# Loading v through GpSimd's casting queue into two padded operands, and one more half batch in seven products

## The chip, the cores and the metric

The kernel runs on one core of one Trainium2 chip. The metric is the device time of one execution in microseconds (us); smaller is better. The kernel before was timed three times: 272.16, 272.57 and 272.89 us, median 272.57 us. One further execution was recorded by the hardware profiler, and all profile lines in this document come from such recordings.

## The reference

Two layers follow each other. The first is a linear attention with cosine and sine weights over 8 batches, 8 heads, 576 positions and 64 values for each head. The second is a two-matrix network with a squared ReLU.

```python
q_p, k_p = phi(q), phi(k)                  # relu(x)*cos(pos) beside relu(x)*sin(pos): 64 -> 128 values
kv  = einsum('bhsf,bhsd->bhfd', k_p, v)    # sums over the 576 positions
z   = sum(k_p, axis=2)
num = einsum('bhsf,bhfd->bhsd', q_p, kv)
den = einsum('bhsf,bhf->bhs', q_p, z) + 1e-06
x   = (num / den) as [4608 tokens, 512]
out = (relu(x @ w_in) ** 2) @ w_out        # 512 -> 2048 -> 512
```

Inputs and output are float32. On the chip the matrix products take bfloat16 and sum in float32.

## The kernel before, in words

**Staging.** A batch has 512 main positions (four blocks j of 128) and a tail of 64. For each batch, q and k are loaded as float32 into one buffer `kq`. VectorE (DVE) or ScalarE (ACT) makes the features, eight instructions for each batch (cos and sin for four blocks j, q and k at once); `fe` holds them in bfloat16. TensorE sums the products of the key features with v in `mm_kv`; its second operand is v with a column of ones beside each head's 64 values (so z comes out with kv), padded to 66 columns: `vext` for the main positions, `vextt` for the tails. The sums are copied to `kvz`. The query features are turned by DMA transposes (`qT_dma`), `mm_num` multiplies them with `kvz`, `div` divides, and DMA transposes (`x_dma`) turn the result into `xT`, the network's input. Batches 0 and 1 are turned by TensorE instead.

**The network.** A batch's 512 main tokens are taken in two halves of the 2048 hidden columns, `gg` 0 and 1, each of two groups `s` of 256. Each can be done plainly (`plan_plain1`: four products `H<batch>.<group>.<token half><hidden half>` of eight matmuls for each group, in which a product needs one token half of `xT` only) or in seven products (`plan_gemm1`: `G<batch>.<group>.P1` to `P7` of four matmuls each). The seven products work on sums of input blocks (`xs`, DVE) and of weight blocks (`w1s`), and each group has seven evictions from PSUM (`seed`, `u2`, `s5`, `c11`, `c12`, `c22`, `c21`) where the plain form has four. P1 needs both token halves. A pair of output blocks is made in seven products as well (`Y<batch>.P1` to `P7`). Before, `PLAIN` names three halves for the plain form: both of batch 1, and the first of batch 2. The tails of all batches are the ninth block, `G8` and `Y8`.

**v before.** For batches 3 to 7, SyncE's queue (SP) loads v as float32 into a staging buffer (`vs`, one slot, in two halves of four heads, in rows of 1 KB; `vst` for the tail). Then ACT or DVE casts each half into the single `vext` (`spread_v`, operations `vs<batch>.0` to `.2`). Batch 2 is loaded by GpSimd's queue (POOL), which can cast, into a bfloat16 staging buffer, and copied to `vext`. As there is one `vext`, the spread of a batch waits until the sums of the batch before have read it.

**Order.** A long table (`ORDER`) gives one order of all operations; each engine and each queue runs its own operations in that order and waits where it must. A star puts an operation on ACT. A planner in the kernel (`Plan.run`) goes through the table with a cost for each operation and picks buffers; the table itself was made outside. Operations of the table that matter here: `ldk`, `ldq`, `ldv` (loads), `kv<b>` (the sums of batch b), `qTd<b>.<i>` and `xTd<b>.<i>` (DMA transposes on SP), `sin<b>.<j>` and `cos<b>.<j>` (features).

The end of the kernel is `Y8`: the last product `P21`, one copy `c111` of 128x256 from PSUM by DVE, and two small stores, one by SP and one by ACT's queue.

Of the kernel before, what the change touches and what calls it, by code (L numbers as in the profile page):

```python
# [35 lines left out]
xT1.2 xTc1.2 Y0.a12 ldk2 Y0.a13 Y0.a14 Y0.b12 Y0.b13 w2t3 xT1.0 xTc1.0 Y0.a15 xTc1.1* vs2.0*
num1.3 Y0.b14 div1.3 Y0.c01* Y0.b15 Y0.c10* Y0.c11 Y0.c00* cos2.1 ldqt3 sin2.0 H1.3.00.0 sin2.1
cos2.3 xT1.3 xTc1.3* sin2.3 ldqt2 H1.3.00r* H1.2.00.0 H1.2.00r* ldkt2 H1.2.10.0 ldv2.1 vs2.1
H1.1.10.0 H1.1.11.0 H1.1.00.0 cos2.0* sin2.2* H1.0.11.0 H1.1.11r* H1.0.01.0 cos2.2* H1.1.00r*
ldkt3 sin2.tk* H1.2.10r* H1.3.10.0 H1.0.11r H1.3.10r* H1.2.01.0 Y0.st1 H1.1.10r* H1.0.01r  # L40
cos2.tk kv2 w2t2 w2t4 H1.1.11q H1.3.10q* kvz2* H1.2.01r* H1.0.10.0 H1.0.10r Y0.st0 qTd2.0
H1.1.01.0 H1.1.01r H1.1.10q H1.3.00q* H1.0.00.0 H1.0.00r* qTd2.1 num2.1 div2.1 H1.2.11.0
H1.3.11.0 ldv3.0 num2.2 H1.2.11r* ldv3.2 H1.1.00q* H1.3.01.0 H1.3.11r* H1.1.01q H1.3.01r* Y1.P10
ldk3 vs3.2* div2.2 H1.3.11q H1.3.01q ldq3 num2.3 div2.3 Y1.seed Y1.P11 Y1.S1 Y1.seed1 Y1.P20
num2.0 div2.0 vs3.0* Y1.P21 Y1.c111* Y1.S2 Y1.S3 cos3.1* ldv4.2 Y1.P5 cos3.0 sin3.0* sin3.1
sin3.2 xTd2.1 num1.4 cos3.3* Y1.P6 H2.1.10.0 Y1.u2 H2.0.11.0 sin3.3* cos3.2 H2.1.10r* Y1.P7
div1.4 ldv3.1 H2.0.11r* Y1.S4 vs4.2* vs3.1* xT1.4 xTd2.0 xs2.1 H2.0.00.0 xs2.3 H2.1.00.0 xs2.2
kv3 xTc1.4* H2.0.01.0 H2.1.00r xs2.4 Y1.c110* H2.0.00r* H2.1.00q* Y1.s5* G2.2.P1 H2.0.01r* kvz3
Y1.c22 G2.2.seed qTd3.0 num3.0 div3.0 cos3.tq* sin3.tq H2.1.11.0 H2.1.11r* H2.1.11q H2.0.10.0
H2.0.10r* num3.1 qTd3.1 H2.1.01.0 div3.1 Y1.P3 num3.2 H2.1.10q* ldq4 w1s3 G2.2.P2 Y1.c12  # L50
H2.1.01r* H2.1.01q* G2.2.P6 G2.2.c11r* div3.2 ldv4.0 G2.2.u2 G2.2.P5 G2.3.P1 ldk4 num3.3 div3.3
vs4.0* qTd3.2 ldkt4 G2.3.P5 G2.2.P7 G2.3.seed G2.2.s5* G2.2.c22r xTd3.0 G2.3.P2 G2.3.P6 G2.3.s5*
G2.3.P3 ldv4.1 G2.2.P4 G2.2.P3 G2.3.u2 G2.3.c11r* G2.3.P7 cos4.3 num3.4 G2.3.c11q Y2.P1 cos4.0
sin4.1* G2.2.c21r* G2.3.c22r G2.2.c12r sin4.0 cos4.1* cos4.2* G2.3.P4 G2.3.c21r xTd3.1 ldv5.2
G2.3.c12r sin4.2 xs3.1 sin4.3* ldkt5 Y1.st0 Y1.P4 Y2.seed G2.3.c21q* G2.3.c22q* G2.3.c12q Y2.S1
G3.0.P1 G3.0.seed qTd4.0 Y1.c21* qTd4.1 Y2.P2 G3.0.P2 xs3.2 G3.0.c11r* G3.0.P5 xs3.3 G3.1.P1
G3.0.P6 G3.0.s5* cos4.tk* G3.1.P5 Y2.S2 G3.0.u2* div3.4 G3.0.P3 Y2.P6 sin4.tk* vs4.1 kv4
G3.0.c12r Y2.u2 G3.1.seed G3.1.P2 Y2.S3 ldk5 G3.1.P6 vs5.2* kvz4* Y2.c11* Y2.S4 G3.0.P7 num4.0
G3.0.c22r ldv5.0 G3.1.c11r* G3.1.c11q* Y2.P5 xs3.4 G3.0.P4 G3.2.P1 div4.0 ldq5 G3.1.u2* G3.1.s5*
ldqt5 vs5.0* Y1.st1 G3.0.c21r num4.2 div4.2 G3.1.P3 Y2.s5 G3.1.P7 G3.1.c22r G3.1.c12r Y2.P7  # L60
num4.1 div4.1 ldqt6 G3.2.seed ldv5.1 G3.1.P4 G3.1.c21r* G3.2.P6 G3.2.u2* ldqt4 G3.2.P2 G3.2.c11r
sin5.0 Y2.c22 Y2.P3 Y2.c12 cos5.3* num4.3 G3.2.P5 G3.3.P1 G3.3.P5 cos5.1* xTd4.0 div4.3 xTd4.1
G3.2.s5* G3.3.seed G3.2.P7 G3.2.c22r G3.2.P3 G3.2.c12r sin5.1 G3.3.s5* G3.3.P6 Y2.st0 G3.3.u2*
cos5.0 qTd5.0 G3.3.P2 G3.3.c11r* G3.3.c11q G3.2.P4 G3.3.P3 G3.3.P7 Y2.P4 G3.3.c22r vs5.1* sin5.3
cos5.2 G3.1.c12q* G3.3.P4 Y3.P1 G3.1.c21q* G3.3.c21r G3.3.c12r G3.3.c12q sin5.2* kv5 xs4.1
G3.2.c21r* G3.3.c21q xs4.2 G4.0.P1 G4.0.P5 qTd5.1 ldv6.0 G3.3.c22q* Y3.seed Y3.P2 cos5.tq*
sin5.tq* kvz5* G3.1.c22q Y3.S1 Y3.S2 xs4.3 num5.0 div5.0 xs4.4 G4.0.seed G4.0.P2 G4.0.s5* ldv6.2
G4.0.P3 Y2.c21* G4.1.P1 G4.0.c11r* G4.0.P6 G4.0.u2* G4.0.c12r ldk6 Y3.S4 Y3.P6 ldq6 G4.1.seed
G4.1.P2 G4.1.c11r* G4.0.P7 G4.1.P6 G4.1.u2* G4.0.c22r vs6.2* num5.2 Y3.S3 G4.1.P5 G4.2.P1
Y3.c11* G4.0.P4 G4.1.P7 G4.1.s5* div5.2 Y3.P5 G4.1.c22r G4.1.c22q num5.3 div5.3 G4.1.P4 G4.1.P3  # L70
G4.0.c21r* G4.1.c12r Y3.u2* G4.2.seed G4.2.P6 G4.2.P2 vs6.0* G4.1.c21r* num5.1 G4.2.u2*
# [12 lines left out]
Y4.c22 G5.3.P1 G5.3.seed num5.4 cos7.0 G5.2.P7 Y4.P3 sin7.1 G5.2.c22r Y4.c12 G5.3.P2 G5.3.c11r*
G5.3.P6 G5.3.u2 div5.4 vs7.1 G5.3.P5 G5.2.P4 xTd6.0 xTd6.1 G6.0.P1 ldv7.2 G5.3.s5* G5.3.P7
G5.3.c22r G5.3.P3 G5.1.c21q* G5.3.c12r Y4.P4 G5.2.c21r* G5.3.P4 G5.1.c12q sin7.3* vs7.2*
G6.0.seed Y4.c21 xs6.1 xs6.2 kv7 G6.0.P2 G6.0.P5 G6.1.P1 kvz7 qTd7.0 num7.0 xs6.3 xs6.4 G6.0.P6
G5.3.c11q* G6.0.s5* G6.0.P3 G6.1.seed G6.1.P2 G6.1.P6 G5.3.c21r* G6.0.c11r* div7.0 G6.1.c11r
G6.0.u2* G6.0.c12r G5.3.c12q* num7.1 Y5.P1 sin7.tq qTd7.1 G6.1.P5 div7.1 G6.1.u2 G6.0.P7
G6.0.c22r xTd5.2 num7.2 div7.2 G6.2.P1 G5.3.c21q* Y5.seed G6.1.s5* G5.3.c22q* Y5.P2 Y5.S1 Y5.S2  # L90
Y4.st0 G6.0.P4 G6.1.P7 G6.0.c21r Y4.st1 Y5.c11* G6.1.c22r cos7.tq qTd7.2 num7.3 G6.1.P3 div7.3
Y5.P5 G6.1.c12r G6.2.seed G6.2.P2 G6.2.c11r* G6.2.P6 xTd7.1 Y5.S4 xTd7.0 Y5.S3 G6.1.P4 G6.2.u2*
Y5.s5* G6.2.P5 G6.1.c21r* G6.2.s5* Y5.P6 G6.3.P1 G6.2.P7 Y5.u2* Y5.P3 G6.2.P3 G6.1.c22q*
G6.3.seed G6.3.P6 G6.3.P2 G6.3.c11r* G6.2.c22r G6.1.c21q Y5.P7 G6.3.u2* G6.3.P5 G6.2.c12r
G6.3.P7 G6.3.c11q Y5.c12 G6.2.P4 G7.0.P1 G6.1.c11q G6.3.s5* G6.3.P3 Y5.c22 Y5.P4 G6.3.c22r
G6.3.c22q G6.3.c12r G6.3.P4 xs7.1 G6.2.c21r* xs7.2 G7.0.seed G7.0.P2 G7.0.c11r xs7.3 Y6.P1
Y5.st0 Y5.c21 xs7.4 G7.0.P5 G7.1.P1 G7.0.s5 G6.1.c12q* G6.3.c12q* Y6.S1 G6.3.c21r* G6.3.c21q*
# [185 lines left out]
def kernel(  # L283
# [189 lines left out]
    def att_bufs(b):  # L473
        kq[b] = buf("kq", [P, 2, H, J, D], F32, "kq")
        vtype = BF16 if b < 3 else F32
        for i in range(2):
            vs[b, i] = buf("y" if b == 1 else "vs", [P, HH, J, D], vtype, "vs")
# [1144 lines left out]
```

## Time and profile before

| | |
|---|---|
| median of three runs | 272.57 us |
| profiled execution, its own time | 271.95 us |
| span of the profiled execution | 269.9 us |
| TensorE busy in the span | 263.1 us, 97% |
| VectorE, ScalarE, GpSimd busy | 228.1, 186.7, 26.9 us |
| granted TensorE clock | 1.0 |

The span is the time between the first and the last instruction; the profiled execution's own time is 2.05 us longer. Queues are written as engine names with a q: SPq is the queue that SyncE issues into. In the page's strips the span is cut into 40 slices of 6.75 us, and a digit is the busy share in tenths. A group's row gives the instruction, what it writes and reads, how often it runs, its busy time with the mean of one in ns, and the idle time just before it. A DMA row gives the time from issue to landing. The matmul of 256 columns has a duration of 273 ns, but matmuls overlap: sixteen that follow each other take 1.75 us in the chain of work, 0.109 us each.

### The profile page before, as it was taken

Reading aid. Unit: us, or ns where it says so; the run is one execution under the profiler, and the core shown is the slowest. Engines: PE = TensorE matmul, PEld = TensorE weight load, DVE = VectorE, ACT = ScalarE, POOL = GpSimd, SP = SyncE. Lnnn points to the kernel's source line nnn. Section 1 sums busy time; section 2 is a strip of 40 time slices with the busy share of each in tenths; the row PEclk is TensorE's granted clock in tenths of the full one; section 3 lists DMA queues with packets and bytes.
Section 4 is the critical chain, followed back from the end, with each engine's and each line's share of the span. In section 5 each row is a group of like instructions: output and inputs, shape, how many; then the busy total and the mean of one; then the engine's idle time right before and its main releaser. Section 6 shows DMA issues by size and latency. Waiting matters only on the chain.

```text
span 269.9 us, 6751 instructions
## 1 busy us (share of the span) xinstructions
PE 263.1 (97%) x2787; PEld 225.0 (83%) x2792; DVE 228.1 (85%) x412; ACT 186.7 (69%) x289; POOL 26.9 (10%) x44
## 2 busy tenths in 40 slices
PE   8899999999999999999999999999999999999994
PEld 3568856699899889989998998899888888888883
DVE  3877987889998999999999999899978858797941
ACT  4762695698888997689699868587658636755510
POOL 8934443200000000000000000000000000000000
PEclk9999999999999999999999999999999999999999
DMA  6999999999899999999899998652540111010115
GB/s 221 220 206 253 328 198 250 298 295 298 221 247 314 221 261 298 300 183 231 284 275 209 232 359 208 152 155 100 61 125 15 38 63 78 8 72 2 78 50 186
DMA packets 82367, 51.23 MB, mean 190 GB/s; under 512 B 53217, under 2 KB 78817, under 8 KB 82337
## 3 DMA queue, kind: packets, MB, share of 16 engines
q1 hardware_dynamic: 71008, 38.28, 55.5%
q0 software_dynamic: 10736, 12.00, 21.2%
q10 hardware_dynamic: 592, 0.52, 0.6%
q8 instruction: 22, 0.36, 0.6%
q14 instruction: 9, 0.07, 0.1%
HBM read 36.70 MB, written 9.44 MB: 171 GB/s over the span
## 4 chain that ended last, share of the span: by engine, by line
PE 83%; DMA 12%; POOL 3%; issue 0%; DVE 0%; POOLq 0%
PE ya L461 18%; PE yb L461 16%; PE hb L461 13%; PE ha L461 8%; PE hc L461 8%; PE hps L461 8%; DMA w1sb<-in_moe_w_in_dram 5%; DMA kq<-in_k_dram 4%; PE num L461 3%; DMA w2sb<-in_moe_w_out_dram 3%; PE kz L461 3%; PE yc L461 3%; PE yh L461 3%; POOL kq L509 1%; POOL w1sb L411 1%; POOL v L1378 1%
## 5 line engine op out<-in xcount | busy, mean ns | idle before, releaser
L461 PEld LDWEIGHTS <-w1sb 128*128 128x128 bf16 x736 | 70.4, 98 | 8.6
L461 PEld LDWEIGHTS <-gs 128*128 128x128 bf16 x512 | 49.9, 98 | 5.8
L461 PEld LDWEIGHTS <-gT 128*128 128x128 bf16 x448 | 43.1, 98 | 9.8 <-issue 0.2
L442 ACT ACTIVATE gT<-gT 128x1024 bf16<-128x1024 bf16 x38 | 39.5, 1059 | 3.4 <-DVE gT L455 1.8
L461 PE MATMUL hps<-xT,w1sb 128*128 128x256 bf16 x320 | 37.4, 273 | 0.0
L448 ACT ACTIVATE fe<-kq,cols 128x1024 bf16<-128x1024 f32 (+1 forms) x39 | 35.1, 950 | 2.8 <-DMA kq<-in_k_dram 1.7
L461 PEld LDWEIGHTS <-w1s 128*128 128x128 bf16 x312 | 29.7, 98 | 3.3
L461 PE MATMUL ya<-w2sb,gT 128*128 128x256 bf16 x256 | 30.7, 273 | 0.0
L461 PE MATMUL hb<-xs,w1sb 128*128 128x256 bf16 x208 | 30.6, 273 | 0.0
L450 DVE TENSOR_SCALAR fe<-kq,cols 128x1024 bf16<-128x1024 f32 (+1 forms) x41 | 26.9, 690 | 4.0 <-DMA kq<-in_k_dram 4.0
L461 PE MATMUL ha<-xT,w1sb 128*128 128x256 bf16 x176 | 26.2, 273 | 0.0
L444 DVE TENSOR_TENSOR gT<-gT 128x1024 bf16<-128x1024 bf16 x34 | 23.2, 686 | 1.2 <-ACT gT L436 0.8
L436 ACT ACTIVATE gT<-ha 128x512 bf16<-128x512 f32 x21 | 12.6, 601 | 15.9 <-PE ha L461 15.9
L633 DVE TENSOR_TENSOR xp<-num,den 128x512 bf16<-128x512 f32 (+1 forms) x33 | 22.2, 675 | 1.1
L436 ACT ACTIVATE gT<-hps 128x512 bf16<-128x512 f32 x26 | 15.4, 602 | 8.1 <-PE hps L461 8.0
L455 DVE CUSTOM_DVE_ANT_0 gT<-hb,s 128x512 bf16<-128x512 f32 x26 | 17.8, 686 | 3.7 <-PE hb L461 3.3
L458 DVE TENSOR_TENSOR gs<-gT 128x2048 bf16<-128x2048 bf16 x16 | 19.4, 1219 | 0.4
L455 DVE CUSTOM_DVE_ANT_0 gT<-hc,u 128x512 bf16<-128x512 f32 x26 | 17.7, 683 | 0.8 <-PE hc L461 0.8
L432 ACT COPY hb<-ha 128x512 f32<-128x512 f32 x26 | 15.2, 585 | 4.3 <-DVE gT L438 1.8
L461 PE MATMUL hb<-xs,w1s 128*128 128x256 bf16 x104 | 15.6, 273 | 0.0
L436 ACT ACTIVATE gT<-hb 128x512 bf16<-128x512 f32 x18 | 10.8, 599 | 7.0 <-PE hb L461 4.5
L461 PE MATMUL hc<-xs,w1s 128*128 128x256 bf16 x104 | 15.6, 273 | 0.0
(120 smaller groups left out, 415.7 us busy)
## 6 DMA issues: line engine op xcount, KB each, us to landing
out_dram<-y SPq DMA_DIRECT2D x16, 512.0 KB, 3.7
vs<-in_v_dram SPq DMA_DIRECT2D x10, 512.0 KB, 4.8
kq<-in_k_dram SPq DMA_DIRECT2D x5, 1024.0 KB, 7.1
kq<-in_q_dram SPq DMA_DIRECT2D x5, 1024.0 KB, 9.2
w1sb<-in_moe_w_in_dram POOLq DMA_DIRECT2D x4, 512.0 KB, 11.6
w2sb<-in_moe_w_out_dram POOLq DMA_DIRECT2D x4, 512.0 KB, 10.3
kq<-in_q_dram POOLq DMA_DIRECT2D x2, 1024.0 KB, 11.2
kq<-in_k_dram POOLq DMA_DIRECT2D x2, 1024.0 KB, 11.1
```

The source lines that it names most:

```text
L411: nc.gpsimd.dma_start(out=w1sb[:, :, f0:f1], in_=moe_w_in[:, f0:f1].rearrange("(kb p) f -> p kb f", p=P),)
L432: (nc.scalar.copy if e == "ACT" else nc.vector.tensor_copy)(out=out, in_=in_)
L436: nc.scalar.activation(out=out, in_=in_, func=ACTF.Relu)
L442: nc.scalar.activation(out=out, in_=in_, func=ACTF.Square)
L444: nc.vector.tensor_tensor(out=out, in0=in_, in1=in_, op=ALU.mult)
L448: nc.scalar.activation(out=out, in_=in_, func=ACTF.Relu, scale=col)
L450: nc.vector.tensor_scalar(out=out, in0=in_, scalar1=0.0, scalar2=col, op0=ALU.max, op1=ALU.mult)
L455: nc.vector._custom_dve(dve_ops.TENSOR_ADD_SAT, out=out, in0=in0, in1=in1, s0=BIG, s1=0.0)
L458: nc.vector.tensor_tensor(out=out, in0=in0, in1=in1, op=op)
L461: nc.tensor.matmul(out=out, lhsT=lhsT, rhs=rhs, start=start, stop=stop, skip_group_check=True)
L509: eng.dma_start(out=kq[b][:, "kq".index(nm)][:, hs, js], in_=main_of(nm, b)[:, hs, js])
L633: nc.vector.tensor_tensor(out=x, in0=n4[:, :, :, 0:D].rearrange("p b (k l) d -> p b k l d", l=2), in1=r.rearrange("p b (k l) -> p b k l", l=2)
```

## The change

- v of batches 2 to 7 is no longer staged. GpSimd's queue reads float32 from HBM and writes bfloat16 straight into the padded operand. A half is now two blocks j with all heads, one DMA for each block (128 partitions, 8 heads, 64 values), so a half is two DMAs. The tail goes into `vextt` in the same way.
- There are two main operands, `vext0` and `vext1`, used in turn as the planner gives them. The staging pool is gone, and with it the 18 spreads `vs2.0` to `vs7.2`.
- `PLAIN` loses (2, 0): the first hidden half of batch 2 runs as `G2.0` and `G2.1`, in seven products.
- The last copy `c111` is cut in two: columns 0 to 127 on DVE (`c111l`), 128 to 255 on ACT (`c111r`); both stores wait for both.
- The second-matrix sum `w2t1` waits for two of the four weight loads instead of four.
- The table is new throughout. SP's queue has 43 plain DMAs instead of 58 (its 30 transposes stay), GpSimd's 62 instead of 35. The tail loads of q and k of batches 2 and 3 change places too.

```diff
-PLAIN = ((1, 0), (1, 1), (2, 0))
+PLAIN = ((1, 0), (1, 1))
...
-    pool("vs", 1, 4096)
...
-    plan.pool("ve", 1)
+    plan.pool("ve", 2)
...
+    vxs = [
+        sb.tile([P, J, H, E1 + 1], BF16, name=f"vext{i}", tag=f"vx{i}", bufs=1) for i in range(2)
+    ]
+    vx = vxs[0]
...
     def load_v(b, i, eng):
-        if i < 2:
+        if b > 1:
+            if i < 2:
+                for j in (2 * i, 2 * i + 1):
+                    src = main_of("v", b)[:, :, j]
+                    eng.dma_start(out=vxs[ve[b].slot][:, j, :, 0:D], in_=src)
+            else:
+                src = v[b, :, MAIN:S, :].rearrange("h p d -> p h d")
+                eng.dma_start(out=vxt[sides[b % 2], b % 2, :, 0:D], in_=src)
+        elif i < 2:
             src = main_of("v", b)[:, i * HH : (i + 1) * HH]
...
-                f"ldv{b}.{i}",
-                {eng: 0.6 if eng == "SP" else 0.95},
+                f"ldv{b}.{i}",
+                {"POOL": 2.0 if i < 2 else 0.95},
...
+            if last and t:
+                h = n // 2
+                parts = [
+                    ("l", {"DVE": dve(h)}, slice(0, h)),
+                    ("r", {"ACT": act(h)}, slice(h, n)),
+                ]
```

The two tables around the point where batch 2 enters the network (before, then after):

```
... num2.0 div2.0 vs3.0* Y1.P21 Y1.c111* Y1.S2 Y1.S3 cos3.1* ldv4.2 Y1.P5 cos3.0 sin3.0* sin3.1
sin3.2 xTd2.1 num1.4 cos3.3* Y1.P6 H2.1.10.0 Y1.u2 H2.0.11.0 sin3.3* cos3.2 H2.1.10r* Y1.P7
div1.4 ldv3.1 H2.0.11r* Y1.S4 vs4.2* vs3.1* xT1.4 xTd2.0 xs2.1 H2.0.00.0 xs2.3 H2.1.00.0 ...

... num2.0 div2.0 sin3.3* Y1.P21 Y1.c111* Y1.S2 Y1.P5 sin3.0* ldv3.0 w1s3 Y1.c110* cos3.1* num1.4
div1.4 Y1.P6 xT1.4 Y1.u2* xTd2.1 cos3.0* xTd2.0 sin3.1 G2.0.P1 G2.0.seed xTc1.4 xs2.1 xs2.2 xs2.4
sin3.2 cos3.3* Y1.P7 ldv4.0 ldqt3 cos3.2 G2.0.P6 G2.0.u2* G2.0.P5 G2.0.P2 xs2.3 G2.0.P7 ...
```

More of the change, by code (lines that the diff above doesn't have):

```diff
@@ L42 @@
[L42 to L59, printed above, removed]
@@ new lines @@
+w2t3 H1.2.00r* H1.1.11q* H1.0.01.0 H1.0.01r* Y0.st0 H1.3.10.0 H1.1.01r* H1.3.10r* w2t2 H1.3.00r*
+H1.0.00.0 kv2 H1.1.10r* H1.1.00.0 H1.1.01q w2t4 kvz2* H1.3.10q H1.0.00r H1.3.00q* qTd2.0 num2.1
+div2.1 qTd2.1 H1.1.10q H1.1.00r* H1.1.00q* Y1.S3 H1.2.01.0 H1.2.01r* H1.3.11.0 H1.3.11r*
+H1.2.11.0 H1.2.11r* num2.2 div2.2 H1.3.01.0 H1.3.01r* H1.3.01q* Y1.P10 Y1.seed H1.3.11q num2.3
+div2.3 ldq3 ldk3 Y1.P11 ldv4.2 Y1.P20 ldqt2 Y1.S1 Y1.seed1 num2.0 div2.0 sin3.3* Y1.P21 Y1.c111*
+Y1.S2 Y1.P5 sin3.0* ldv3.0 w1s3 Y1.c110* cos3.1* num1.4 div1.4 Y1.P6 xT1.4 Y1.u2* xTd2.1 cos3.0*
@@ new lines @@
+xTd2.0 sin3.1 G2.0.P1 G2.0.seed xTc1.4 xs2.1 xs2.2 xs2.4 sin3.2 cos3.3* Y1.P7 ldv4.0 ldqt3
+cos3.2 G2.0.P6 G2.0.u2* G2.0.P5 G2.0.P2 xs2.3 G2.0.P7 G2.0.s5 G2.0.P3 G2.0.c22r G2.0.c12r
+G2.0.c11r* G2.1.P1 G2.1.seed Y1.S4 G2.0.P4 Y1.s5 G2.1.P5 G2.1.s5* G2.1.P2 G2.1.c11r* G2.1.c11q
+G2.1.P6 G2.1.u2* ldv3.1 G2.0.c21r* kv3 kvz3* qTd3.0 G2.1.P7 G2.1.c22r G2.1.P3 cos3.tq* num3.0
+div3.0 qTd3.1 ldk4 sin3.tq* G2.2.P1 G2.1.c12r G2.2.P5 G2.1.c22q* G2.1.P4 ldq4 G2.1.c21r* num3.1
+div3.1 G2.2.seed qTd3.2 Y1.c22 Y1.P3 Y1.c12 G2.2.P2 num3.2 div3.2 G2.1.c12q* G2.1.c21q ldv5.2
@@ L474, in att_bufs @@
         kq[b] = buf("kq", [P, 2, H, J, D], F32, "kq")
-        vtype = BF16 if b < 3 else F32
-        for i in range(2):
-            vs[b, i] = buf("y" if b == 1 else "vs", [P, HH, J, D], vtype, "vs")
-        vs[b, 2] = buf("xpt" if b < 2 else "kqt", [P, HH if b < 2 else H, D], vtype, "vst")
+        ve[b] = buf("ve", None, None, "ve")
+        if b < 2:
+            for i in range(2):
+                vs[b, i] = buf("y", [P, HH, J, D], BF16, "vs")
+            vs[b, 2] = buf("xpt", [P, HH, D], BF16, "vst")
         if b < 2:
@@ L729, in spread @@
                     f"vs{b}.{i}",
-                    both(act(n), d) if i < 2 or b > 1 else both(0.6, 0.3),
+                    both(act(n), 0.06 + 0.0003 * n) if i < 2 else both(0.6, 0.3),
                     lambda e, i=i: spread_v(e, b, i),
-                    [landed[i]] + ([sums_of[max(1, b - 2)]] if i == 2 and b > 1 else []),
-                    [vs[b, i]] + ([] if i == 2 and b > 1 else [ve]),
+                    [landed[i]],
+                    [vs[b, i], ve[b]],
                 )
@@ L1344, in plan_w2_sums @@
                 lambda e, n=n, in0=in0, in1=in1: tt(w2t[n][:, :, :], in0(), in1(), ALU.subtract),
-                w2_in + [made[a] for a in after] + (plain if n == 3 else []),
+                w2_in[: 2 if n == 1 else 4]
+                + [made[a] for a in after]
+                + (plain if n == 3 else []),
             )
@@ L1557 @@
             if b + 1 < B:
-                got, ve = ahead.pop() if ahead else plan_loads(b + 1, "POOL" if b == 1 else "SP")
+                got = ahead.pop() if ahead else plan_loads(b + 1, "POOL" if b == 1 else "SP")
                 if b % 2:
```

226 lines of the change are left out of this document (114 added, 112 removed).

## The prediction

> **What bounds the kernel now.** I read the page's busy times first, then the chain of work, then the sixteen-matmul rows of the chain, to see how full the bounding engine is.
>
> ```profile
> span 269.9 us, 6751 instructions
> PE 263.1 (97%) x2787; PEld 225.0 (83%) x2792; DVE 228.1 (85%) x412; ACT 186.7 (69%) x289; POOL 26.9 (10%) x44
> DMA  6999999999899999999899998652540111010115
> PE 83%; DMA 12%; POOL 3%; issue 0%; DVE 0%; POOLq 0%
> ```
>
> TensorE ends the chain, and VectorE and ScalarE put nothing into it. The DMA share of the chain lies in the first 43 us (weights and the first batches). The DMA strip is full to slice 23, about 158 us. The stage from 60 to 80 us, where the plain half of batch 2 stands, looks so (busy by engine; chain; SyncE's queue; ScalarE):
>
> ```profile
> 60.00:80.00 20.00, 20.00 (x250) 17.99 (x249) 19.44 (x34) 17.01 (x26) 0.00 (x0) 1.00 0.96 255
> ...
> 74.92 0.66 PE yb L461 x6
> 75.57 1.75 PE hps L461 x16
> 77.32 1.75 PE yb L461 x16
> 79.06 0.22 PE tx L656 x4
> ...
> 70.06 1.26 SPq L678 DMA_TRANSPOSE xT<-xp  x1
> 71.43 0.53 SPq L526 DMA_DIRECT2D vs<-in_v_dram  x1
> 72.20 2.20 SPq L678 DMA_TRANSPOSE xT<-xp  x1
> ...
> 71.75 4.27 ACT L448 ACTIVATE fe<-kq,cols 128x1024 bf16<-128x1024 f32 x4
> ```
>
> TensorE has no gap there; VectorE is at 19.44 of 20. Sixteen matmuls take 1.75 us, 0.109 each. So work taken from VectorE and ScalarE buys nothing by itself: only fewer matmuls do, or a shorter end. New waits cost at once, because nothing covers TensorE.
>
> **The change part by part.** *The seven products.* The plain half has 2 groups x 4 products x 8 = 64 matmuls; in seven products it is 2 x 7 x 4 = 56. Eight fewer at 0.109 us: -0.87 us, all on the path. This is the only large saving.
>
> *The spreads.* These rows and the two bfloat16 copies of batch 2 go:
>
> ```profile
> L432 ACT CAST vext<-vs 128x1024 bf16<-128x1024 f32 x6 | 6.3, 1049 | 0.0
> L432 DVE CAST vext<-vs 128x1024 bf16<-128x1024 f32 x4 | 2.7, 685 | 0.0
> L432 ACT CAST vextt<-vst 64x512 bf16<-64x512 f32 x5 | 3.1, 614 | 0.1
> ```
>
> About 14 us of two engines that are not on the chain: 0. It pays for the seven products' evictions: 14 instead of 8 in the half, six more at 0.59 (ACT) to 0.69 us (DVE), 3.5 to 4.1 us, of which the ones that TensorE waits for count. In G2.0 the new order puts P5, P2, P7, P3 in a row, and P3 needs P5's bank copied out: cover 2 x 0.44 = 0.87 us, copy 0.69 plus two handoffs. Bounds: 0 (the rows of the seven-product groups show no idle TensorE) to one uncovered copy in each of two groups, 1.4 us. I take 0.3, nearer the rows.
>
> *The loads of v.* Before, a half is 512 rows of 1 KB on SP's queue; after, it is 2 x 128 x 8 = 2048 pieces of 256 B read and 128 B written, on GpSimd's queue. No row shows this transfer (none writes rows 132 B apart), but the tail loads of v at the start write 128 B pieces with a cast. The DMA view of 7.2 to 7.8 us:
>
> ```profile
> DMA packets 487, 0.11 MB, mean 178 GB/s; under 512 B 461, under 2 KB 476, under 8 KB 487
> q0 software_dynamic: 487, 0.11, 177.3%
> ```
>
> 0.6 us x 16 engines / 487 = 20 ns a packet by rate; 1.77 of them overlap, so 35 ns each if they did not. A half costs 2048/16 x 20 = 2.5 us by rate, at most 4.5. A half before is 512 KB; hardware packets average 0.555 x 269.9 x 16 / 71008 = 34 ns for all sizes, so 512/16 x 34 = 1.1 us or somewhat more. For a batch: about 5.0 instead of 2.2 to 3, some 2 to 3 us more on DMA engines that are full until 158 us. GpSimd's issue is free (its `kq` loads of as many pieces take 0.92 us each, and it has nothing else to do). Two operands let v come a batch earlier, so kv itself should not wait for v: batch 2's last half is issued near 48 us, behind k and q (k landed at 53.4), and 2.5 + 0.6 + 2.5 us later is 59, before kv2 (60.3, and 0.87 later in the new order). What matters is what these packets push back. After kv2 GpSimd is free to issue three halves (v3 twice, v4), 7.5 us, together with k3 and q3 on SP and just before xTd2.
>
> *Where batch 2 enters.* Before, the first product needs one token half (xTd2.1) and the other is first read at 79.29. After, G2.0.P1 follows Y1.P6 and the four tail transposes, and needs both. Arrival: 74.92 + 0.66 + 0.22 = 75.8 us. The two landings before:
>
> ```profile
> xT<-xp SPq DMA_TRANSPOSE x1, 2.8
> ...
> xT<-xp SPq DMA_TRANSPOSE x1, 4.9
> ...
> kq<-in_q_dram SPq DMA_DIRECT2D x1, 1024.0 KB, 9.2
> ```
>
> The later one was issued at 72.20 and landed at 77.1, behind the load of v that stood between them and now doesn't. If it lands as the first, 75.0: no wait. If as before, 1.3 us. Ahead of it in time are k3 and q3 (2 x 2.2, at 34 ns for each KB) and 7.5 us of v, all from about 61 us: until 73 or 74 at full use, so it competes with the last of them. I take 0.8 (bounds 0 and 1.3, more if v costs 4.5 a half, see below). There is a rule on this: the Trainium skill, "DMA: Bandwidth & Descriptors", section "Issuing engines are not separate DMA queues", says that the DMAs of all issuing engines run on the same 16 DMA engines and interleave. By that rule the 0.8 stands; were the queues separate paths, it would be 0 and the sum -0.3. The strip of before cannot tell the two apart.
>
> *The features of batch 3* move ahead of Y1's evictions on ScalarE: sin3.3, c111, sin3.0, c110, cos3.1, u2. Y1.P7, now right after G2.0.P1 (76.2), needs u2. q3 landed at 61.93 + 9.2 = 71.1; three features at 1.07, two copies at 0.37, u2 at 0.59 give 75.7. Covered by 0.5 us, so 0; each us that q3 lands later than 71.6 is a us of TensorE. Two loads of v less stand ahead of it on SP, three halves more on the other queue.
>
> *The end.* c111 on DVE was 0.42 us:
>
> ```profile
> 264.95 2.19 ACTq L1106 DMA_DIRECT2D out_dram<-y  x3
> 266.09 0.42 DVE L432 COPY y<-ya 128x256 f32<-128x256 f32 x1 [0.45 <-PE ya L461]
> ```
>
> ScalarE's part must stand behind that queue's second store, which was being issued until about 266.5, as DVE's copy ended. ACT copies 256 columns in 0.375 and 512 in 0.587 us, so 128 in about 0.27. The last stores go 0.26 later instead of 0.13 earlier (DVE's half alone). I take +0.26.
>
> *SP's queue* loses 15 issues of about 0.5 us in front of transposes, and the moved tail loads are 0.6 each: 0, no row has TensorE waiting for an issue there. Later batches: G3.0.P1 stands behind xTd3.1, which followed a v load that is gone from its queue, with 5 more us of v on the other: 0, bounds 0 and 2. w2t1, second memset: 0, the weights land as before.
>
> Sum: -0.87 + 0.3 + 0.8 + 0.26 = +0.5 us. On the profiled execution's own 271.95 that is 272.4; it lies 0.6 below the median of 272.57, on which I put it: 273.1 us.
>
> **The rivals.** *The packets are the bound (slower).* If 128 B pieces at 132 B steps cost 35 ns, three halves take 13.4 us; with 4.4 of k3 and q3 from 61 us they end near 79, and xTd2.0 with them: TensorE waits about 3 us instead of 0.8, and perhaps again after kv3, where four more such loads are issued beside k4 and q4. For it: the full strip to 158 us. Against: overlap of 1.77 in the row. 275 us, up to 277. It decides from about 27 ns a packet.
>
> *ScalarE's head of line, or the lock between VectorE and GpSimd (slower).* q3 at 73 instead of 71.1 costs 1.4 us through u2. And this row says that GpSimd's issue can hold VectorE:
>
> ```profile
> L450 DVE TENSOR_SCALAR fe<-kq,cols x14: 467/484/977, 5.0 to 40.4; 128x512 bf16<-128x512 f32 x14
> ```
>
> One feature took 977 instead of 484 ns, at the start, where GpSimd issues without pause. Two or three such in the 60 to 80 us stage, where VectorE has 0.56 us to spare, give 1 to 1.5 us. Either: 273.9 to 274.5. The Trainium skill, "SBUF — State Buffer", section "Who interferes with whom", makes it a rule: a VectorE operation in a two-port mode and a GpSimd operation block each other for a whole instruction. Against it stands where the issues fall: mostly after kv2, kv3, kv4, while the features follow later.
>
> *Faster.* The load of v that stood before xTd2.0 is gone, the transpose lands by 75.0, no group waits: -0.87, and with the end at +0.26 or -0.13 it is 271.6 to 272.0. It decides from xTd2.0 landing before 75.8. Against: three halves of v in flight just then.
>
> **How the numbers follow.** A difference of about 0.3% (0.82 us) is what a measurement of this kernel can tell from no change. Forecast, the saving eaten by small waits: 0.43, 272.0 to 273.4. Packets: 0.22, 274 to 277. ScalarE's line 0.12 and the lock 0.10, 273.4 to 274.5. Faster by over 0.3%: 0.13, as all waits must vanish and the end too must not grow. So slower 0.44, same 0.43, faster 0.13. The range 271.9 to 275.3 leaves out the best of the faster case and the worst of the packets.
>
> **What would show it.** TensorE's matmuls 8 fewer; `hps` 256, `ha`, `hb`, `hc` more. An idle TensorE ended by the transpose before the first `ha` of batch 2, near 76 us: 0.8. No idle at kv2 to kv7. v's landings 5 to 6 us after issue, 128 B packets near 20 ns by rate. The last DVE and ACT copies 0.4 us apart. The forecast is wrong if TensorE waits for `kq` features or kv, if DVE features above 750 ns are many, or if packets overlap less than in the row above.

## The result and the profile after

The changed kernel takes 281.24 us (median of four; 280.67 to 281.91) against 272.37 us (four runs of the kernel before beside it, 272.02 to 272.89): 1.033 times the time, interval 1.031 to 1.036. That is 8.9 us more than before; 273.1 had been forecast, with 275.3 as the upper end of the range. In the runs further down the median counts every execution, and the ratio leaves out those that lie more than 1.5% above the fastest of their kernel.

The page of the changed kernel, the lines that answer to those of before (span, busy time, the DMA strip, the chain of work, and one group of part 5):

```profile
span 278.8 us, 6744 instructions
PE 265.9 (95%) x2784; PEld 225.0 (81%) x2784; DVE 228.2 (82%) x409; ACT 179.5 (64%) x282; POOL 49.8 (18%) x71
DMA  7999999999996999999999999358114211200106
PE 90%; DMA 4%; DVE 4%; ACT 1%; issue 0%
L464 PE MATMUL ha<-xT,w1sb 128*128 128x256 bf16 x192 | 29.0, 275 | 6.2 <-DMA xT<-xp 6.2
```

The last line shows where the time went: one idle stretch of TensorE of 6.2 us, ended by the DMA transpose of x, before the first `ha` product of batch 2. The same stretches of the kernel before had TensorE busy throughout. After (us; busy time and count of each engine; granted clock; DMA share; GB/s):

```profile
70.00:76.00 6.00, 6.00 (x72) 5.24 (x72) 5.86 (x11) 3.47 (x6) 0.00 (x0) 1.00 2.16 187
76.00:82.00 6.00, 0.46 (x7) 0.33 (x5) 0.80 (x2) 2.17 (x3) 0.00 (x0) 0.99 1.64 142
82.00:84.00 2.00, 1.38 (x7) 1.00 (x7) 1.26 (x4) 0.33 (x1) 0.00 (x0) 0.50 1.12 207
84.00:86.00 2.00, 2.00 (x15) 1.54 (x14) 1.68 (x4) 1.31 (x2) 0.00 (x0) 0.69 0.00 0
86.00:88.00 2.00, 2.00 (x20) 1.72 (x18) 0.69 (x1) 1.00 (x2) 0.00 (x0) 1.00 0.85 195
```

The reader sees a second loss in the clock column: TensorE comes out of the wait at 0.50 and 0.69 of its clock, and in the four microseconds from 82 to 86 it begins 22 matmuls (38 in a run below that keeps TensorE busy through the wait).

The transposes themselves (DMA rows of the changed kernel, first xTd2.1, issued at 70.27, then xTd2.0, issued at 72.43; the last number is us from issue to landing; 2.8 and 4.9 before):

```profile
xT<-xp SPq DMA_TRANSPOSE x1, 9.4
...
xT<-xp SPq DMA_TRANSPOSE x1, 10.1
```

And what the DMA engines did in the meantime (DMA view of the changed kernel from 72 to 74 us, then from 75 to 77; packets, MB, share of 16 engines):

```profile
DMA packets 2403, 0.31 MB, mean 155 GB/s; under 512 B 2396, under 2 KB 2403, under 8 KB 2403
q0 software_dynamic: 2395, 0.30, 263.3%
q1 hardware_dynamic: 8, 0.01, 1.4%
...
q0 software_dynamic: 823, 0.10, 79.2%
q1 hardware_dynamic: 794, 0.20, 77.5%
```

q0 is GpSimd's queue, q1 SP's. xTd2.1 had been issued by 71.5, and xTd2.0 was being issued from 72.4 on, but from 72 to 74 nearly every packet was one of v's pieces of 128 bytes. The later of k3 and q3, which stand ahead of the transposes on SP's queue, landed at 72.9; in the packet records the first block of the transposes moves at 74.6 us. From 75 to 77 the two queues move about as many packets each, some 400 a microsecond. Alone, the transposes of q in the kernel before move 2066 packets from 77 to 79, 1030 a microsecond.

One thing more lies in this wait. From 77.0 to 78.4 us next to nothing moves on either queue: 29 packets of 128 or 256 bytes that begin between 77.0 and 77.6 last 0.8 to 1.4 us each, where those around them last 0.03. The DMA view from 77 to 78.2:

```profile
DMA packets 134, 0.03 MB, mean 22 GB/s; under 512 B 134, under 2 KB 134, under 8 KB 134
```

So for 1.4 of the 6.3 us the transposes hardly moved, and v did not move either. The packet records of the run with 52 more matmuls show the same from 77.0 to 78.4, those of the run with wider packets from 75.7 to 77.3. What holds the engines then is not known, and none of the theories below has it.

Set against TensorE's own work, the 8.9 us come out so. TensorE is 0.45 us later than before from its first transpose of x on (15.68 instead of 15.23 us); since that one starts anywhere from 15.0 to 15.7 us in the runs of this document, I take this for scatter. It waits 6.3 us at G2.0.P1 (start to start) and loses 1.6 us between there and G2.1.P5, 1.3 of it on the low clock (see the run with 52 more matmuls). Eight matmuls fewer return 0.87. Behind its last matmul stand 4.62 us instead of 3.85, +0.77. The remaining 0.7 us are spread: behind the first 15 us TensorE has no other idle stretch over 0.2 us.

### The profile page after: what moved, and what is told of

The parts are those of the page before. It is cut to its first block, busy times and chain, and to the rows that moved or that the text cites. A ratio compares the mean times of both kernels' runs of the same rounds, so it can differ in the third digit from the quotient of the medians.

```text
span 278.8 us, 6744 instructions
## 1 busy us (share of the span) xinstructions
PE 265.9 (95%) x2784; PEld 225.0 (81%) x2784; DVE 228.2 (82%) x409; ACT 179.5 (64%) x282; POOL 49.8 (18%) x71
## 4 chain that ended last, share of the span: by engine, by line
PE 90%; DMA 4%; DVE 4%; ACT 1%; issue 0%
PE ya L464 16%; PE yb L464 15%; PE hb L464 13%; PE hps L464 10%; PE ha L464 9%; PE hc L464 8%; PE yh L464 5%; DMA xT<-xp 4%; PE num L464 4%; PE wm L464 3%; PE kz L464 3%; PE yc L464 2%; PE tq L658 1%; DVE xp L640 1%; DVE gs L461 1%; DVE fe L453 1%
## 5 line engine op out<-in xcount | busy, mean ns | idle before, releaser
L464 PEld LDWEIGHTS <-w1sb 128*128 128x128 bf16 x704 | 67.5, 98 | 14.6 <-issue 6.3
L451 ACT ACTIVATE fe<-kq,cols 128x1024 bf16<-128x1024 f32 (+1 forms) x44 | 40.3, 959 | 3.8 <-DMA kq<-in_k_dram 3.6
L445 ACT ACTIVATE gT<-gT 128x1024 bf16<-128x1024 bf16 x32 | 33.2, 1055 | 3.3 <-DVE gT L458 3.0
L464 PE MATMUL ha<-xT,w1sb 128*128 128x256 bf16 x192 | 29.0, 275 | 6.2 <-DMA xT<-xp 6.2
L464 PE MATMUL hps<-xT,w1sb 128*128 128x256 bf16 x256 | 29.7, 273 | 0.0
L532 POOL DMA_DIRECT2D vext<-in_v_dram x24 | 21.2, 908 | 34.6 <-PE kz L464 33.7
L447 DVE TENSOR_TENSOR gT<-gT 128x1024 bf16<-128x1024 bf16 x40 | 26.9, 684 | 0.6 <-ACT gT L439 0.3
L453 DVE TENSOR_SCALAR fe<-kq,cols 128x1024 bf16<-128x1024 f32 (+1 forms) x36 | 23.4, 684 | 4.6 <-DMA kq<-in_k_dram 4.6
L435 ACT COPY s<-hc 128x512 f32<-128x512 f32 x24 | 14.0, 586 | 4.4 <-PE hc L464 4.3
L435 ACT COPY u<-hb 128x512 f32<-128x512 f32 x21 | 12.2, 588 | 6.7 <-PE hb L464 6.6
```

The costliest lines, as they stand in the source:

```text
L435: (nc.scalar.copy if e == "ACT" else nc.vector.tensor_copy)(out=out, in_=in_)
L445: nc.scalar.activation(out=out, in_=in_, func=ACTF.Square)
L447: nc.vector.tensor_tensor(out=out, in0=in_, in1=in_, op=ALU.mult)
L451: nc.scalar.activation(out=out, in_=in_, func=ACTF.Relu, scale=col)
L453: nc.vector.tensor_scalar(out=out, in0=in_, scalar1=0.0, scalar2=col, op0=ALU.max, op1=ALU.mult)
L464: nc.tensor.matmul(out=out, lhsT=lhsT, rhs=rhs, start=start, stop=stop, skip_group_check=True)
```

## The experiments

Three theories at first. A: v's small packets on GpSimd's queue hold up SP's DMA transposes. B: any v on GpSimd's queue holds them up, however it is cut. C: v does no harm, the seven products of batch 2 are late by themselves. D came from the clock column: a wait costs a second time. All ratios are to the kernel before, run beside each.

**v alone (e4_v_only).** The new v path in the order of the kernel before; the plain half, the old end and the four weight loads of `w2t1` stay.

```diff
-PLAIN = ((1, 0), (1, 1))
+PLAIN = ((1, 0), (1, 1), (2, 0))
...
-            if last and t:
+            if False:
```

> The v part of the change alone, in the order of the kernel before: v of batches 2 to 7 by GpSimd's queue into the two operands, no spreads, but batch 2's first half in plain products and the end as before; of the table only the spreads go and ldv2.2 moves behind kv1. GpSimd's queue then issues ldv3.1, ldv4.0 and ldv4.1 as soon as kv2 is through, just ahead of xTd2.1. Theory A: TensorE waits about 4.3 us at H2.1.10.0 (needs xTd2.1 alone) and 1 us at H2.0.00.0 (needs xTd2.0), runs on a cold clock behind it, and the time is 277 to 280 us although not one of the seven products is there. Theory C (the seven products are what is late): 272 to 273.5 us.

Measured: 281.83 us, 1.032 (1.028 to 1.037), as much as the whole change and more than the 277 to 280 of A. TensorE's waits for a DMA between 50 and 115 us (total, times, longest):

```profile
PE hps L460 <- DMA xT<-xp: 3.7, 1, 3.7
PE num L460 <- DMA qpT<-fe: 1.8, 2, 1.3
```

So C falls: with batch 2's first half in plain products the transpose of x still costs 3.7 us. The second wait expected, at H2.0.00.0, did not come; instead the transposes of q of the same batch, some 15 us earlier, were late too, which no theory had named.

**The seven products alone (e3_seven).** The kernel before with its own v path, only `PLAIN` changed and the order between Y1.P5 and G2.3.P1 arranged for it.

```diff
-PLAIN = ((1, 0), (1, 1), (2, 0))
+PLAIN = ((1, 0), (1, 1))
```

> The seven products alone: the kernel before with its v path (staged by SP's queue, spread by DVE and ScalarE), but batch 2's first half as two groups of seven products. The order between Y1.P5 and G2.3.P1 is arranged anew for it. Theory A (the loss comes from v's packets beside the transposes): xTd2.0 lands near 77 us as before, TensorE waits 0 to 1.5 us at G2.0.P1, eight matmuls less are -0.87 us, and the time is 271.8 to 273.7 us. Theory C (the seven products, with their need of both token halves and their chains of evictions, are what is late): 276 us or more.

Measured: 273.33 us, 1.0037 (1.0016 to 1.0058). The only wait over 0.3 us of TensorE that the view of waits gives between 50 and 115 us is this:

```profile
PE hc L460 <- DVE xs L457: 0.4, 1, 0.4
```

xTd2.0 landed at 75.48, before G2.0.P1 came (75.53); in this order no load of v stands between the two transposes of x. So the seven products fit, as A says, but they gain nothing: 0.87 us of matmuls are saved, and from the spans (270.7 against 269.9) about 1.7 us of small waits must have come in.

**Two halves of v moved ahead (e1_v3_early).**

```diff
-... H1.0.11r ldv2.0 Y0.st1 ...
+... H1.0.11r ldv2.0 ldv3.0 ldv3.1 Y0.st1 ...
```

> The changed kernel with only the table edited: ldv3.0 and ldv3.1 stand right behind ldv2.0 on GpSimd's queue, so of the three halves that were in flight beside xTd2.1 and xTd2.0 only ldv4.0 is left. Theory A (the two DMA transposes of x wait until the 128-byte packets that GpSimd's queue has in flight are through, so the wait grows with the packets left): TensorE's wait at G2.0.P1 falls from 6.3 us to between 0 and 1.5 us, the cold stretch behind it goes too, and the time is 273.5 to 276 us. Theory B (any v on GpSimd's queue slows SP's queue, however much of it): the wait stays above 4 us and the time above 278 us. Theory C (not the v loads but the seven products, which need both token halves of xT, make batch 2 late): the wait hardly moves, 280 to 282 us.

Measured: 286.04 us, 1.050 (1.045 to 1.054), worse than the change itself. A and C missed the time; B had it (above 278 us), but not the wait of over 4 us at G2.0.P1 that was to make it. The rows tell why. In this run xTd2.1 was issued when nothing of v was in flight any more; its row, and TensorE's waits from 50 to 115 us:

```profile
xT<-xp SPq DMA_TRANSPOSE x1, 2.8
```

```profile
PE num L462 <- DMA qpT<-fe: 3.7, 2, 3.4
PE hc L462 <- DVE xs L459: 3.4, 1, 3.4
PE ha L462 <- DMA xT<-xp: 0.3, 1, 0.3
```

At the place that the run was made for, A was right: 2.8 us as in the kernel before, and a wait of 0.3. But the two halves now ran beside qTd2.0 and qTd2.1, whose landings went from 62.3 and 64.2 us in the changed kernel (60.1 and 61.9 before) to 67.7 and 73.8. SP's queue stood behind them: k3 and q3 were issued 5 us later. And at batch 3 the sums `xs` waited for xTd3.1, which took 11.3 us beside what was left of a tail and three more halves of v. The wait had moved with the packets.

**v held behind the transposes of x (e5_gate).** As above, and v of batch 4 waits for two small copies on GpSimd that read both tiles of `xT`.

```diff
+                def gate(e):
+                    for c in range(2):
+                        nc.gpsimd.tensor_copy(out=gt[:, c : c + 1], in_=xT[2, c][:, 0, 0:1])
...
-... xTd2.0 sin3.1 G2.0.P1 ...
+... xTd2.0 sin3.1 gate2 ldv4.0 ldv4.1 G2.0.P1 ...
```

> The changed kernel with v kept away from the transposes of batch 2: ldv3.0 and ldv3.1 stand right behind ldv2.0, and ldv4.0 and ldv4.1 behind two one-column copies on GpSimd that read both tiles of xT of batch 2, so nothing of v is in flight while xTd2.1 and xTd2.0 run. The seven products and the end are as in the changed kernel. Theory A: no wait at G2.0.P1 (under 1 us) and no cold stretch; 272.4 less 0.87 us of matmuls, plus 0.45 us at the start, 0.77 us at the end and 0.3 to 0.8 us at batch 2 gives 273.0 to 274.3 us. Theory B: the wait shrinks too, so this run does not tell it from A; theory C: 278 us or more.

Measured: 285.52 us, 1.049 (1.045 to 1.053). xTd2.1 took 2.8 us again, the wait for `xT` at batches 2 and 3 is 0.7 us in two parts, and the loss stands at the transposes of q (4.2 us for `qpT`, 3.4 us for the tails' `qpTt`) and at xTd3.0, which took 11.5 us beside batch 5's v. A's price for the place was right, its time not: it had left out that the packets must go somewhere.

**v between the transposes (e8_gates, e9_gates_end).** GpSimd reads a column of both `qpT` of batches 2, 3 and 4 before it issues the next batch's v.

```diff
-... qTd2.1 H1.1.10q ...
+... qTd2.1 gate2 ldv3.0 ldv3.1 H1.1.10q ...
...
-... qTd3.1 ldk4 ...
+... qTd3.1 gate3 ldv4.0 ldv4.1 ldv4.2 ldk4 ...
...
-... qTd4.1 G3.1.u2 ...
+... qTd4.1 gate4 ldv5.0 ldv5.1 ldv5.2 G3.1.u2 ...
```

> The changed kernel with v between the transposes: GpSimd reads one column of both qpT of batches 2, 3 and 4 before it issues the two halves of the next batch's v, so v of batch 3 starts when qTd2.1 has landed and not beside xTd2, v of batch 4 behind qTd3.1, v of batch 5 behind qTd4.1. Theory A: xTd2.1 takes 2.8 to 4 us from issue to landing instead of 9.4, the wait at G2.0.P1 is under 2 us, qTd3.2 and xTd3.0 come up to 2 us later than in the kernel before because batch 4's v runs beside them; 272.5 to 275.5 us. Theory B (GpSimd's queue as such): no change, 280 us or more.

Measured: 286.1 us, 1.047 (1.039 to 1.054). The time that B gave came, and A's did not. xTd2.1 took 7.4 us and TensorE waited 2.4 us for xTd2.0, because v of batch 3 was still in flight: both halves, issued from 64.0 to 67.5, landed only at 73.5 and 74.9, since beside k3 and q3 they hardly move. The clearest row is from 117 to 119 us of this run, v of batch 5 beside loads of k, q (1 KB packets) on SP's queue:

```profile
q1 hardware_dynamic: 413, 0.42, 81.0%
q0 software_dynamic: 260, 0.03, 25.2%
```

Beside 1 KB packets v gets 130 packets a microsecond; alone it gets 1200 (2395 in 2 us, above). So the v issued at 112.4 to 116.6 lands from 124.7 to 129.2, and then stands beside xTd4, after which TensorE waits 2.6 us for the sums `xs` of batch 4. So v does not only hold up transposes, as A has it; it is also held up itself, by the large packets of SP's loads. Whether that is the small packets or the second queue, this run does not tell; the pair of runs on queue and packet size takes them apart.

The other run adds `Y1.P7` ahead of `G2.0.P1`, and the old end:

```diff
-... Y1.P6 xT1.4 Y1.u2* xTd2.1 cos3.0* xTd2.0 sin3.1 G2.0.P1 ... Y1.P7 ...
+... Y1.P6 Y1.u2 xT1.4 Y1.P7 xTd2.1 cos3.0* xTd2.0 sin3.1 G2.0.P1 ...
...
-            if last and t:
+            if False:
```

> As the run with v between the transposes, and two things more: Y1.u2 on DVE and Y1.P7 ahead of G2.0.P1, so that TensorE has 1.7 us of other work while xTd2.0 comes, and the last eviction and the last stores in one piece and in the order of the kernel before. The tail behind TensorE's last matmul goes from 4.6 back to 3.85 us (-0.75), the wait at G2.0.P1 to nearly nothing: 0.7 to 2 us less than that run, 271.3 to 274 us. If the tail's 0.77 us were noise between runs, only the first part shows.

Measured: 284.87 us, 1.046 (1.039 to 1.053). The time was missed by as much as in the run before; the difference, 1.2 us in the medians, is no more than noise, as the two intervals nearly coincide. The two parts came as said: no wait for `xT` over 0.25 us is left at batch 2 (2.4 us in the run before; 1.2 us now stand at batch 3), and the tail behind the last matmul went from 4.60 to 3.83 us.

**The packets made larger (e2_wide).** The three halves beside xTd2, each as one DMA.

```diff
+            if (b, i) in ((3, 0), (3, 1), (4, 0)):
+                flat = vxs[ve[b].slot].rearrange("p j h e -> p (j h e)")
+                dst = flat[:, i * 1056 : i * 1056 + 1024].rearrange("p (h c) -> p h c", h=HH)
+                src = main_of("v", b)[:, i * HH : (i + 1) * HH]
+                eng.dma_start(out=dst, in_=src.rearrange("p h j d -> p h (j d)"))
```

> The changed kernel, but the halves (3,0), (3,1) and (4,0) of v are each one DMA that reads rows of 1 KB and writes them with the cast as 512 bytes, as 512 packets instead of 2048; bytes, queue, place and issue order are the same. The values land in the wrong places of the operand and overwrite its column of ones, so the output of the later batches is not the reference's. Theory A (the number of small packets sets the wait): the wait at G2.0.P1 falls from 6.3 to below 2.5 us and the time to 274 to 277 us. Theory B (what counts is the bytes, or only that GpSimd's queue is busy beside SP's): the wait stays at 5 to 6.5 us, 279.5 to 282 us.

Measured: 278.75 us, 1.021 (1.017 to 1.025); the wait at G2.0.P1 is 3.2 us, xTd2.1 takes 8.3, xTd2.0 7.2 instead of 10.1. That lies between what A and B gave, so neither holds as it was put: a quarter of the packets at the same bytes halves the wait. What makes the rest is not shown; the standstill of the DMA engines from 75.7 to 77.3 us lies in it.

**Queue and packet size apart (e10_queue, e14_narrow).** The kernel before, plain half, staging and spreads included. In the first run v of batches 3 to 7 comes by GpSimd's queue as bfloat16, 512 bytes in a row; in the second in four DMAs a half, 128 bytes in a row.

```diff
-        vtype = BF16 if b < 3 else F32
+        vtype = BF16
...
-                {eng: 0.6 if eng == "SP" else 0.95},
+                {"POOL": 0.95},
```

> The kernel before, with one thing changed: v of batches 3 to 7 comes by GpSimd's queue with the cast into the staging buffer, as v of batch 2 does there already, instead of by SP's queue as f32; the write to SBUF has 512 bytes in a row instead of 128, and DVE and ScalarE spread it as before. Theory A (the 128-byte packets are what holds the transposes up): 272 to 274.5 us, waits of TensorE at batch 2 and 3 under 1.5 us together. Theory B (v on a second queue beside SP's k, q and transposes, whatever its packets, comes late or makes them late): 277 us or more, as in the run with the v part alone (281.8).

```diff
-            eng.dma_start(out=vs[b, i][:, :, :, :], in_=src)
+                for j in range(J):
+                    eng.dma_start(out=staged(b, i)[:, :, j], in_=src[:, :, j])
```

(`staged` is the same buffer with its blocks j outermost, for batches 3 to 7; the spread reads it so.)

> As the run with v on GpSimd's queue into the staging buffer, but each half of batches 3 to 7 written by four DMAs, one for each j, 128 bytes in a row as in the changed kernel (2048 packets a half instead of 512); still one half in flight at a time, since there is one staging buffer, and the spreads stay. It fills the table of halves in flight beside xTd2 (three or one) against bytes in a row (128 or 512). If the size of the packets alone holds the transposes up: xTd2.1 takes 6 us or more from issue to landing (3.9 with 512 bytes, 9.4 in the changed kernel) and TensorE waits 2 us or more at batch 2; 278 us or more. If it takes both, many halves in flight and small packets: xTd2.1 takes 3.5 to 5.5 us, batch 2 hardly waits, and the time is 275.5 to 278 us, the spreads that come late included.

Measured: 275.74 us, 1.014 (1.008 to 1.021), and 282.29 us, 1.039 (1.034 to 1.044). The first time lies between A's and B's. With 512 bytes the transposes of x of batch 2 are held up little (xTd2.1 3.9 us, xTd2.0 5.0; 2.8 and 4.9 before), and TensorE does not wait for them, so the queue alone does not make the wait at batch 2. With 128 bytes xTd2.1 takes 3.7 and xTd2.0 5.1 us, so small packets alone, one half at a time, don't make it either. But in these runs the half is issued 1.2 and 2.2 us behind xTd2.1, where in the changed kernel all three halves were issued ahead of it: the number of halves in flight and their place ahead of the transposes are not told apart. My second reading for that run was right on the transposes and wrong by 4 us on the time. Both runs lose elsewhere. ScalarE before and at the spread of batch 5's first half, 512 bytes first, then 128 (start, duration, instruction, idle time before it):

```profile
113.92 1.05 ACT L432 COPY vext<-vs 128x1024 bf16<-128x1024 bf16 x1 [3.51 <-DMA vs<-in_v_dram]
```

```profile
119.84 1.05 ACT L432 COPY vext<-vs 128x1024 bf16<-128x1024 bf16 x1 [6.31 <-DMA vs<-in_v_dram]
```

In the kernel before the same half was loaded by SP in 4.8 us and its spread began at 110.31 with no wait. On GpSimd's queue it took 8.9 us beside k5 and q5, in small packets 10.9, so here the larger part of v's delay comes with the queue and the smaller with the packets' size. ScalarE runs in order, so the evictions behind the spread wait, and TensorE for them (3.8 us in one piece in the second run).

**The wait filled with work (e7_dummy).** The changed kernel with 52 matmuls into a bank that is overwritten.

```diff
+            def fill(e):
+                for _ in range(DUMMIES):
+                    mm(c[:, 0, :], ident[:, :], w1_block(0, 0)[:, 0, 0:W], True)
```

> The changed kernel with 52 matmuls of 128x256 ahead of G2.0.P1 whose result is overwritten (about 5.7 us at 0.109 us each), so that TensorE works while it would wait for xTd2.0; loads and transposes are as in the changed kernel. Theory D (the wait costs a second time, since TensorE comes out of it on a low clock, 0.50 and 0.69 in the four microseconds behind): the granted clock behind the wait is 0.95 or more, matmuls there are 0.11 us apart instead of 0.21, and the time falls by 0.9 to 1.3 us, to about 280 us. Rival (those matmuls are slow for another reason, their data or the packets still running): spacing and time do not change.

Measured: 282.02 us, 1.034 (1.031 to 1.037); it did not get faster. The same two stretches behind the wait, and TensorE's waits at batch 3, 96 to 114 us (the view gives none there for the changed kernel):

```profile
82.00:84.00 2.00, 1.72 (x17) 1.39 (x15) 1.23 (x4) 0.72 (x2) 0.00 (x0) 1.00 1.13 206
84.00:86.00 2.00, 2.00 (x21) 1.80 (x19) 1.80 (x5) 1.40 (x2) 0.00 (x0) 1.00 0.00 0
```

```profile
PE hc L463 <- DVE xs L460: 1.3, 1, 1.3
PE yb L463 <- DVE gs L460: 1.2, 1, 1.2
```

The clock is 1.00 and 38 matmuls begin instead of 22. Between G2.0.P1, which starts at the same time in both (82.6), and G2.1.P5 TensorE now loses 0.3 us instead of 1.6: D is shown, the low clock costs 1.3 us. The time did not fall all the same. kv3 starts 1.2 us earlier, v of batches 4 and 5 is issued that much earlier, and xTd3.1, issued 1.2 us earlier, lands 1.45 us later (107.95 instead of 106.50). What was won went into the next collision, with the 2.5 us of waits above. In the changed kernel xTd3.0 and xTd3.1 took long as well (8.1 and 6.3 us; 4.2 and 5.9 before), but there TensorE came to batch 3 too late to wait for them.

**The end (e12_split, e13_endorder).** The kernel before, first with only the copy in two halves, then with only the new order of products and stores.

```diff
-... Y8.P21 Y8.c111 Y8.st0110 Y8.st0100
+... Y8.P21 Y8.c111l Y8.c111r Y8.st0110 Y8.st0100
```

> The kernel before, with only the last eviction (c111 of the last pair) in two halves, DVE and ScalarE, and the order as before. The prediction's step: ScalarE's half stands behind ScalarE's issue of a store, the tail behind TensorE's last matmul grows from 3.85 by 0.26 us, to 4.1 us. Rival (the split costs nothing or gains, and the 0.77 us of the changed kernel's tail come from the new order of the last stores): tail 3.6 to 3.9 us.

```diff
-... Y8.P7 Y8.c12 Y8.st011 Y8.c22 Y8.st001 Y8.st111 Y8.st101 Y7.P4 Y7.c21* Y7.st1 Y8.P4 Y8.c21* ...
+... Y8.P7 Y8.c22 Y8.c12 Y7.P4 Y8.P4 Y8.st111 Y8.st101 Y8.st011 Y7.c21* Y7.st1 Y8.c21* Y8.st001 ...
```

> The kernel before, with only the order of its last stores and of the products between them as in the changed kernel (P4 of the last two groups back to back, the stores of the upper half behind them), the last eviction in one piece. If the order makes the tail: 4.4 to 4.7 us behind TensorE's last matmul instead of 3.85. If it is the split: 3.8 to 4.0 us.

Measured: 272.60 us, 1.0012 (0.9997 to 1.0027), and 273.73 us, 1.0049 (1.0030 to 1.0069). The tails are 4.22 and 5.54 us. The last copies of the first of the two:

```profile
266.18 0.29 DVE L430 COPY y<-ya 128x128 f32<-128x128 f32 x1 [0.45 <-PE ya L459]
266.69 0.27 ACT L430 COPY y<-ya 128x128 f32<-128x128 f32 x1 [1.67 <-DVE y L430]
```

ScalarE's half begins 0.5 us behind VectorE's, when its queue's second store has been issued: the split alone costs 0.37 us of tail. The order alone costs 1.7, more than I had given it: four stores of SP stand in a row (2.62 us of issuing in that run, 3.71 in the changed kernel). With the split and the new order together, in the changed kernel, the tail is 4.62; so the two do not add up, and why the split makes the new order's tail shorter was not tried. Each tail is that of one profiled execution; the medians (0.5 and 1.6 us above the kernel before beside them) agree with them.

No run here beats the kernel before, and nothing in them points to a version that would: the seven products add about twice what they save, and the direct load makes TensorE wait for the DMA engines, while what it saves on VectorE and ScalarE shortens nothing, as they are not the bound.

## Why the prediction was wrong

- **The saving (-0.87) and the spreads (0)** hold. That the spreads are gone even protects the changed kernel: kv2 to kv7 never wait, and no evictions stand behind a late v, as they do in the two staged runs on GpSimd's queue.
- **The step that failed is "where batch 2 enters"**: 0.8 us, bounds 0 and 1.3. Measured: 6.3 us, and 1.3 us more for the low clock, for which the prediction had no term. The upper bound was only the landing of before, 77.1 us; xTd2.0 landed at 82.6. The price of v by itself was not the fault: 2395 packets in 2 us are 13 ns a packet by rate, below the 20 I used, so a half is 1.7 us where nothing else runs, and not 2.5. But v landed 9.7 us after its issue (the median of the page), where I had 5 to 6. The fault was to add up amounts of traffic and let everything end when the sum is through (73 or 74 us). I took "interleave" to mean that each transfer gets its share of time. The rows show something else: v gets few packets beside 1 KB ones (260 in 2 us), runs ahead alone when those are through (2395 in 2 us), and the transposes begin late and then get about half of the packets (794 of 1618). The Trainium skill, "DMA: Bandwidth & Descriptors", section "Queues, rings and completion order", says that an engine goes round its queues a packet at a time, where a packet holds several descriptors. The 823 against 794 packets from 75 to 77 us agree with such turns, though they don't show how long a turn is. I had cited another section of that page, which says only that they interleave, and drew the milder conclusion. The standstill from 77.0 to 78.4 us is a part of the 6.3 that no sum of traffic would have given.
- **"The packets are the bound"**, my rival on this side (0.22, 274 to 277 us), named the place and the sign. Its condition, over 27 ns a packet, was not met (13 by rate), and its 3 us were half of what came: it came near by a price that did not hold.
- **The evictions (0.3, at most 1.4).** The seven products alone, in an order arranged for them, gave about 1.7 us of small waits by the difference of the spans: above my upper bound. That turns the gain of 0.87 into the 0.9 us loss of that run.
- **The end (+0.26).** The split alone gave 0.37, near enough. But I priced one instruction and not the order of the stores, which costs 1.7 us alone and 0.77 together with the split.
- **Later batches (0, bounds 0 and 2)** came out at 0 for a wrong reason: TensorE came to batch 3 late. In the run with 52 more matmuls, where it came 1.2 us earlier and the transposes up to 1.45 us later, there are 2.5 us of waits.
- **ScalarE's head of line and the lock.** The later of k3 and q3 landed 1.7 us later than before, 72.86 instead of 71.15. The bigger wait lies over it, so its cost was not measured. VectorE's one feature between 60 and 80 us took 744 ns against 745 before: no sign of a lock there.
- **SP's issues (0)** and GpSimd's issues (24 at 0.9 us, with nothing behind them but loads) held, but for the stores at the end of the kernel.

Open: why the transposes' first block moved 3.1 us after xTd2.1's issue had ended, and 1.7 us after k3 and q3 had landed. GpSimd's packets were running in all runs with such a delay, but no run tells whether the transposes were waiting for their turn or for something of their own. Open as well: what the standstill of all queues is, and whether it is the number of halves or their place ahead of the transposes that counts.

## What to carry to other kernels

Do not price a second DMA queue by its bytes or by its packets times a rate: see which transfers are in flight together. Here a transfer of 128-byte pieces crawled beside 1 KB packets and then stood in the way of the transposes behind them. A load that is taken off the queue that the transposes use also loses its place in that queue's order; moving it by hand, ahead or behind, only moved the collision, in all four runs that tried it. And where TensorE has no cover, cost a long wait twice, once for itself and once for the clock behind it (6.2 us without work, and 1.3 us more).

## What the runs showed of the hardware

- Packets a microsecond of 16 engines: 128-byte pieces with a cast on GpSimd's queue 1200 alone, 410 beside a DMA transpose, 130 beside 1 KB loads. Transposes 1030 alone, 400 beside such pieces. In those two microseconds the two queues together did 810 a microsecond, fewer than either alone.
- xTd2.1, the same DMA transpose in every run, took 2.8 to 3.6 us with no half of v on GpSimd's queue, 3.7 and 3.9 us with one half issued 1.2 to 2.2 us behind it, and 7.4 to 9.4 us with two or three halves issued ahead of it. It does not take v to make a transpose slow: in the changed kernel the one issued at 167.40 us took 8.5 us with no v in flight, behind a load of q and a store on its own queue. Nor does one half always leave it fast: with 512-byte pieces, the one issued at 142.21 us took 7.7.
- In the packet records of every run, the kernel before too (151.1 to 152.4 us), there are stretches of some 1 to 2 us in which a dozen or more small packets, which otherwise last some 0.03 us, last 0.7 us or more, and the queues move little (22 GB/s in the view from 77 to 78.2 us above). Their cause is open.
- Out of 6.2 us without work TensorE came with a granted clock of 0.50 in the first two and 0.69 in the next two microseconds, which cost 1.3 us. The Trainium skill, "TensorE: Matmul & The Clock Gate", Part 1, tells of half the clock after at least one idle window of some 3.4 us, and of about as long at work to get back. The rows agree on the half and on the way back: 0.50 for two microseconds and a mean of 0.69 over two more are some 3.2 us at half. The mean of 0.99 from 76 to 82 us puts the fall near 82, over 5 us after TensorE had run out of work.
